# Fourier sums formed pair by pair at the end of the recurrence, and the first pair's MLP recorded ahead of the other pairs' mixing

## The chip, the cores and the metric

The kernel runs on one core of a Trainium2 chip. The metric is the device time of one execution in microseconds (us); of several executions the median is quoted. Runs of one call share a chip and the runs of the kernel before, and the three chips on which the experiments ran gave the kernel before as 784.95, 784.61 and 789.55 us, so times are compared within a chip, as ratios.

## The reference

The reference is a DeltaNet recurrence (4 batches, 8 heads, 768 steps, head size 48), followed by an FNet block on the joined heads (rows of 384): a two-dimensional Fourier transform, its real part added to the input, a normalization and an MLP of width 1536. All data are fp32.

```python
def _attn_ref(q, k, v, beta):
    k_n = k / (np.linalg.norm(k, axis=-1, keepdims=True) + 1e-06)
    state = np.zeros((B, H, D, D))
    for t in range(S):
        y[:, :, t] = einsum(q_t, state)
        v_old = einsum(state, k_t)
        state = state + b_t * outer(k_t, v_t - v_old)
# ... rows of the heads side by side: x is (4, 768, 384)
def _moe_ref(x, w_ch1, w_ch2):
    X = np.fft.fft(np.fft.fft(x, axis=1), axis=2)
    u = x + np.real(X)
    un = (u - mean(u)) / sqrt(var(u) + 1e-06)
    return u + np.maximum(un @ w_ch1, 0.0) @ w_ch2
```

## The kernel before

The sequence is cut into chunks of 64 steps, 12 chunks for each batch. Step `m` of the program does one chunk of the recurrence (`chain(m)`). Beside the recurrence run two generators: `pre` prepares the next group of chunks (transposes `pt`, products `pg`, then the triangular inversion on VectorE, which starts with a 1024-column transpose `X<-A`), and `side` does the Fourier mixing and the MLP of the batch before. Every fourth chunk begins a "quad"; a group is two quads.

Batch 0's rows lie in three tile pairs `x[T]`, each with two tiles of 128 rows. `fourier(b)` folds the pairs to sums and differences, transforms along the sequence (`pf`), along the features (`pb`), adds the result to the rows, and takes the statistics. `mlp(b)` normalizes a pair (`un`), transposes it (`ptr`, then `unT`), and multiplies by the first weight (`ph`) and the second (`po`).

Matmul results of all these stages, `pf`, `pb`, `pd`, `pt`, `ptr`, `ph` and `po`, lie in PSUM tiles of one tag, which has two buffers:

```python
def ps_one(shape, name):
    return ps.tile(shape, F32, tag="one", bufs=2, name=name)

def fourier(b):
    x = xs[b]
    F = wk.tile([128, 2, 2, S // 2], F32, tag="F", name="F")
    scr = wk.tile([128, 6 * (HD + 1)], F32, tag="scr", name="scr")
    for a in range(2):                     # part 0: sums, part 1: differences
        eo = scr[...]
        for T in range(TH):
            dve.tensor_tensor(eo[:, T], x[T][:, 0], x[T][:, 1], op=op)
        # ... fold along the features into ed (GpSimd for part 0), then six short sums z in scr
        yield
        for i in range(2):
            pf = ps_one([128, 512], "pf")
            # ... 24 matmul records for a part, z by stab
            act.activation(F[0:rows, a, i]..., pr, ACT.Copy)
    for T in range(TH):
        pb = ps_one([128, DM], "pb")
        # ... 4 matmuls, F by dtab
        for t, op in enumerate((ALU.subtract, ALU.add)):
            # ... four additions of pb to x[T][:, t]
        yield
        # ... (last pair: pd), bn_stats, bn_aggr, rstd
        norms[b, T] = mv, rstd
        yield

def mlp(b, groups):
    def transposed(g):
        # ...
        for tt in range(GT):
            dve.tensor_scalar(un, x[g][:, tt, :], mv[...], rstd[...], op0=ALU.subtract, op1=ALU.mult)
            pt = ps_one([128, KD, 128], "ptr")
            for dt in range(KD):
                tr(pt[:, dt, :], un[:, 128 * dt:128 * dt + 128], dt == 0)
            act.activation(unT[:, :, 128 * tt:128 * tt + 128], pt, ACT.Copy)
        return unT
    unT = transposed(groups[0])
    yield
    # ... ph, hT, po

def second(b):
    # ... batch 0:
        w = second_weight()     # fetches, converts and joins w2, slice by slice
        advance(w)
        run(fourier(b))         # the whole mixing of batch 0 is recorded at once
        mixed.add(b)
        yield
    channels = mlp(b, ...)
    if b == 0:
        for _ in range(KF + 1):
            advance(channels)
            advance(w, 2)
            yield
        run(w)
    yield from channels
```

The loop over the steps, where `side` is turned before `pre` and so the mixing is recorded before the first transposes of the preparation:

```python
    for m in range(NCH, STEPS):
        # ...
        for i, _ in enumerate(chain(m)):
            # ...
            if n == 0 and i == 1:
                run(side, *later)
                later.clear()
                side = second(b - 1)
            if m > NCH or i > 0:
                due[0] += 4.6 if g == 1 else PRE
                due[1] += SIDE[b]
            while max(due) >= 1.0:
                for i, gen in ((1, side), (0, pre)):
                    if due[i] >= 1.0:
                        due[i] -= 1.0
                        advance(gen)
```

## Time and profile before

| | kernel before |
|---|---|
| time | 788.09 us median of 3 runs (787.66 to 789.56) |
| span in the profile | 784.7 us |
| TensorE (PE) | 89% of the span |
| VectorE (DVE) | 48% |
| ScalarE (ACT) | 33% |
| rows of batch 0 complete | 147.2 us |
| products of the mixing (`pb`) | from 161.79 us |
| first transposes of the preparation (`pt`) | 172.17 us |
| first product with the first weight (`ph`) | 180.31 us |
| inversion starts (`X<-A`, 1024 columns) | 193.11 us |

The prediction below shows the main lines of this profile. It does not show the granted clock of TensorE in the 40 slices, which matters later; in this row a 9 is full speed or nearly so, and a slice is 19.6 us:

```profile
PEclk9999999989998999699999999899999999999999
```

The windows of the same kernel around the mixing (stretch, length, then busy us and count of PE, PE's weight loads, DVE, ACT and POOL; then granted clock, DMA share, GB/s):

```profile
158.00:165.00 7.00, 6.98 (x56) 5.62 (x56) 3.18 (x12) 2.05 (x3) 0.00 (x0) 1.00 0.28 73
165.00:174.00 9.00, 5.46 (x71) 3.82 (x70) 8.94 (x34) 2.48 (x5) 1.88 (x4) 0.82 0.28 89
174.00:182.00 8.00, 7.24 (x79) 5.51 (x81) 7.17 (x18) 6.06 (x17) 1.53 (x2) 0.78 0.37 67
```

While DVE adds (8.94 of 9 us), PE waits, and its clock falls to 0.82. And in the timeline (start, length, engine, operation, count) the products of the three pairs lie close together, with a wait of the preparation behind them:

```profile
161.79 3.46 PE L131 MATMUL pb<-dtab,F 128*128 128x193 f32 x16
166.12 1.76 PE L131 MATMUL pb<-dtab,F 128*128 128x193 f32 x8
```

A pair has 8 records of `pb`, so the first line is pairs 1 and 2 back to back and the second line is pair 3.

### The profile page before, as it was taken

How to read it: one execution, taken by the hardware profiler on the slowest of the kernel's cores; microseconds unless marked ns; L12 is line 12 of the kernel's file. 1: busy time of each engine (PE TensorE's matmuls, PEld its weight loads, DVE VectorE, ACT ScalarE, POOL GpSimd, SP SyncE). 2: the span in 40 equal slices, each digit the busy share in tenths (PEclk: the TensorE clock that was granted, in tenths of full speed). 3: DMA queues.
4: the chain of work that ended last, by engine and by line, in shares of the span. 5: the costliest groups of instructions: out<-in, count | busy, mean ns of one | idle time of the engine just before them, and what ended most of it. 6: DMA issues, size and time to landing. Idle time of an engine off the chain costs nothing.

```text
span 784.7 us, 17842 instructions
## 1 busy us (share of the span) xinstructions
PE 699.9 (89%) x7640; PEld 513.0 (65%) x7640; DVE 379.4 (48%) x952; ACT 260.0 (33%) x634; POOL 58.7 (7%) x83
## 2 busy tenths in 40 slices
PE   5852799989988997999989998999999989999997
PEld 4531687867656765786666775776767666677684
DVE  2699766575992598245961119783111146100000
ACT  3741354227436404532152540315312121021120
POOL 8020000010000001010100001010000010100000
PEclk9999999989998999699999999899999999999999
DMA  8651033225320212001202101001000000000000
GB/s 189 163 113 31 7 85 57 46 74 123 87 69 9 38 32 43 16 10 25 50 6 42 32 2 42 1 1 32 12 12 11 12 11 1 20 1 20 11 11 20
DMA packets 82447, 30.75 MB, mean 39 GB/s; under 512 B 77392, under 2 KB 78928, under 8 KB 82368
## 3 DMA queue, kind: packets, MB, share of 16 engines
q1 hardware_dynamic: 78224, 22.31, 13.8%
q0 software_dynamic: 1968, 6.91, 2.7%
q8 instruction: 60, 0.98, 0.5%
q10 hardware_dynamic: 2176, 0.39, 0.3%
q14 instruction: 19, 0.16, 0.1%
HBM read 24.87 MB, written 4.72 MB: 38 GB/s over the span
## 4 chain that ended last, share of the span: by engine, by line
PE 48%; DVE 10%; ACT 5%; issue 3%; DMA 0%; SPq 0%; POOL 0%; POOLq 0%; DVEq 0%; ACTq 0%
PE ph L131 20%; PE po L131 15%; DVE X L131 3%; PE pc L131 3%; DVE A L131 2%; PE pf L131 2%; PE pj L131 2%; ACT A L131 2%; PE pb L131 2%; ACT wt L131 1%; PE pg L131 1%; PE py L131 1%; DVE sm L131 1%; DVE x L131 1%; PE pt L131 1%
## 5 line engine op out<-in xcount | busy, mean ns | idle before, releaser
L131 PE MATMUL ph<-unT,w 128*128 128x256 f32 x864 | 213.8, 395 | 4.5 <-ACT unT L131 2.0
L131 PE MATMUL po<-w,hT 128*128 128x384 f32 x576 | 202.2, 498 | 1.7 <-ACT KQT L131 0.7
L131 PEld LDWEIGHTS ph<-unT,w 128*128 128x128 f32 x864 | 160.3, 193 | 33.7 <-ACT hT L131 3.7
L131 PEld LDWEIGHTS po<-w,hT 128*128 128x128 f32 x576 | 105.7, 191 | 68.2 <-issue 1.5
L131 ACT ACTIVATE hT<-ph 128x256 f32<-128x256 f32 x144 | 54.9, 383 | 179.6 <-PE ph L131 179.3
L131 DVE TENSOR_TENSOR x<-x,po 128x384 f32<-128x384 f32 x24 | 13.2, 552 | 112.5 <-PE po L131 112.4
L131 ACT ACTIVATE U<-pc 128x192 f32<-128x192 f32 x48 | 15.9, 331 | 110.0 <-PE pc L131 98.4
L131 ACT ACTIVATE KQT<-pt 128x256 f32<-128x256 f32 (+1 forms) x82 | 32.0, 419 | 44.9 <-PE pt L131 44.3
L131 PEld LDWEIGHTS pc<-U,wt 64*64 64x64 f32 x768 | 34.0, 163 | 19.7 <-issue 10.3
L131 PE MATMUL pg<-KQT 48*64 48x64 f32 (+1 forms) x1024 | 41.7, 309 | 5.5 <-ACT KQT L131 4.4
L131 PEld LDWEIGHTS pg<-KQT 48*64 48x64 f32 x1024 | 32.1, 178 | 20.4 <-ACT KQT L131 11.2
L131 PE MATMUL pc<-U,wt 64*64 64x48 f32 x768 | 41.2, 253 | 4.7 <-DVE U L131 2.1
L131 DVE TENSOR_TENSOR st<-st,pc 128x192 f32<-128x192 f32 x44 | 15.3, 347 | 61.0 <-PE pc L131 56.8
L131 DVE TENSOR_TENSOR U<-V,pc 128x192 f32<-128x192 f32 x48 | 16.8, 350 | 53.1 <-PE pc L131 52.9
L131 DVE TENSOR_TENSOR A<-X 128x30 f32<-128x30 f32 (+14 forms) x120 | 41.0, 342 | 2.9
L131 DVE TENSOR_TENSOR X<-X,A 128x30 f32<-128x30 f32 (+14 forms) x120 | 39.5, 329 | 2.9
L131 DVE TENSOR_TENSOR x<-x,pb 128x193 f32<-128x193 f32 (+1 forms) x96 | 26.4, 346 | 23.1 <-PE pb L131 23.1
L716 POOL DMA_INDIRECT out_dram<-x,rows_hi x12 | 12.3, 1024 | 335.9 <-DVE x L131 179.9
L131 PE MATMUL pt<-pack,kp 128*128 128x128 f32 x96 | 24.4, 349 | 10.3 <-DMA pack<-k_pack 4.8
L131 PE MATMUL pt<-pack,qp 128*128 128x128 f32 x96 | 23.4, 341 | 11.0 <-DMA qp<-in_q_dram 11.0
L131 PE MATMUL pj<-Z,A 32*64 32x64 f32 x320 | 15.0, 257 | 19.9 <-DVE Z L131 19.6
L131 ACT ACTIVATE A<-pg 128x256 f32<-128x256 f32 (+1 forms) x72 | 25.4, 378 | 21.7 <-PE pg L131 16.6
(125 smaller groups left out, 840.2 us busy)
## 6 DMA issues: line engine op xcount, KB each, us to landing
qp<-in_q_dram SPq DMA_DIRECT2D x96, 48.0 KB, 2.4
V<-in_v_dram SPq DMA_DIRECT2D x96, 48.0 KB, 2.4
kp<-in_k_dram SPq DMA_DIRECT2D x80, 48.0 KB, 2.5
w<-in_moe_w_ch_dram SPq DMA_DIRECT2D x8, 384.0 KB, 3.2
w<-in_moe_w_ch_dram POOLq DMA_DIRECT2D x6, 384.0 KB, 6.4
x<-in_moe_w_ch_dram SPq DMA_DIRECT2D x6, 384.0 KB, 3.7
x<-in_moe_w_ch_dram POOLq DMA_DIRECT2D x4, 384.0 KB, 9.2
out_dram<-x SPq DMA_DIRECT2D x8, 192.0 KB, 2.0
```

The source lines that it names most:

```text
L131: ins = getattr(self.engine, name)(*args, **kwargs)
L716: nc.gpsimd.indirect_dma_start(out=out.rearrange("b s m -> (b s) m"), out_offset=bass.IndirectOffsetOnAxis(ap=rows_hi[:, i:i + 1], axis=0) ...
```

## The change

The intent has three parts. The folds of each pair are formed as soon as the pair's rows are there, in the last steps of the recurrence (which are held in program order), all of them on VectorE, where GpSimd did a part of them before; and both parts (sums and differences) get tiles of their own, so that the second need not wait for the first. The additions after the products are six per pair, not eight. And the MLP of the first pair, its normalization and transposes, is recorded as soon as that pair's statistics are, ahead of the mixing of the other two, so that it can start early.

```diff
+        eds = [F[:, 1 - a].rearrange("p i k -> p (i k)") for a in range(2)]
+        if b == 0:
+            hT = wk.tile([128, KF, GT * 128], F32, tag="hT", name="hT").rearrange("p f t -> p (f t)")
+            zs = hT[:, 0:1158], hT[:, 1158:2316]
+        else:
+            scr = wk.tile([128, 6 * (HD + 1)], F32, tag="scr", name="scr")
+            zs = scr, scr
 ...
+        def folded(a, Ts, helped):       # the folds of the pairs Ts
+        def shifted(a):                  # the six short sums of a part
 ...
+        if b == 0:
+            for T in range(TH - 1, -1, -1):
+                folded(0, [T], False)
+                folded(1, [T], False)
+                if T > 0:
+                    yield
+            mixed_sums = [shifted(a) for a in range(2)]
 ...
+            add(x[T][:, :, 0:HD + 1], pb[:, None, 0:HD + 1].broadcast_to([128, 2, HD + 1]), ALU.add)
+            add(x[T][:, :, HD + 1:DM], pb[:, None, HD - 1:0:-1].broadcast_to([128, 2, HD - 1]), ALU.add)
             for t, op in enumerate((ALU.subtract, ALU.add)):
                 rop = ALU.add if op == ALU.subtract else ALU.subtract
-                add(x[T][:, t, 0:HD + 1], pb[:, 0:HD + 1], ALU.add)
-                add(x[T][:, t, HD + 1:DM], pb[:, HD - 1:0:-1], ALU.add)
 ...
             w = second_weight()
             advance(w)
-            run(fourier(b))
-            mixed.add(b)
-            yield
+            while (b, 0) not in norms:
+                advance(first_mixing)
         channels = mlp(b, list(range(TH if b == B - 1 else TH - 1)))
         if b == 0:
-            for _ in range(KF + 1):
+            advance(channels)            # un, ptr, unT of the first pair
+            run(first_mixing)            # then pairs 2 and 3
+            mixed.add(b)
+            yield
+            for _ in range(KF):
                 advance(channels)
                 advance(w, 2)
                 yield
 ...
+                if m in (10, 11):
+                    advance(first_mixing)
```

The order of the first weight's staging buffers is changed as well, so that the tile which now holds the sums is free in time.

More of the change, by code (lines that the diff above doesn't have):

```diff
@@ L315, in __init__ @@
             un = [wk.tile([128, PW, 2], I32, tag="unT", bufs=2, name="w64") for _ in range(2)]
-            self.stages = [hT[:, i] for i in range(4)] + un + [
-                xpairs[i].rearrange("p t (f two) -> p (t f) two", two=2).bitcast(I32) for i in range(3, 7)]
+            xp = [xpairs[i].rearrange("p t (f two) -> p (t f) two", two=2).bitcast(I32) for i in range(3, 7)]
+            self.stages = xp[0:2] + [hT[:, i] for i in range(4)] + un + xp[2:4]
             self.ops = []
@@ L728, in fourier, with widths @@
         F = wk.tile([128, 2, 2, S // 2], F32, tag="F", name="F")
-        scr = wk.tile([128, 6 * (HD + 1)], F32, tag="scr", name="scr")
-        for a in range(2):
-            op, op2 = (ALU.add, ALU.subtract) if a == 0 else (ALU.subtract, ALU.add)
-            w = HD + 1 if a == 0 else HD - 1
-            o = 1 if a == 0 else 0
-            eo = scr[:, 0:TH * DM].rearrange("p (t d) -> p t d", t=TH)
-            for T in range(TH):
+        eds = [F[:, 1 - a].rearrange("p i k -> p (i k)") for a in range(2)]
[5 more added lines that the diff above has]
+            zs = scr, scr
+            eds = eds[0], eds[0]
+        def widths(a):
+            return (HD + 1, 1) if a == 0 else (HD - 1, 0)
+        def folded(a, Ts, helped):
+            op = ALU.add if a == 0 else ALU.subtract
+            w, o = widths(a)
+            eo = zs[a][:, 0:TH * DM].rearrange("p (t d) -> p t d", t=TH)
+            ed = eds[a][:, 0:TH * w].rearrange("p (t d) -> p t d", t=TH)
+            for T in Ts:
                 dve.tensor_tensor(eo[:, T], x[T][:, 0], x[T][:, 1], op=op)
-            ed = F[:, 1].rearrange("p i k -> p (i k)")[:, 0:TH * w].rearrange("p (t d) -> p t d", t=TH)
-            eng = nc.gpsimd if a == 0 else nc.vector
-            eng.tensor_tensor(ed[:, :, o:o + HD - 1], eo[:, :, 1:HD], eo[:, :, DM - 1:HD:-1], op=op)
+            ts = slice(min(Ts), max(Ts) + 1)
+            eng = nc.gpsimd if helped else nc.vector
+            eng.tensor_tensor(ed[:, ts, o:o + HD - 1], eo[:, ts, 1:HD], eo[:, ts, DM - 1:HD:-1], op=op)
             if a == 0:
-                nc.gpsimd.tensor_copy(ed[:, :, 0:HD + 1:HD], eo[:, :, 0:HD + 1:HD])
-            z = scr[:, 0:6 * w].rearrange("p (i d) -> p i d", i=6)
+                nc.gpsimd.tensor_copy(ed[:, ts, 0:HD + 1:HD], eo[:, ts, 0:HD + 1:HD])
+        def shifted(a):
+            w = widths(a)[0]
+            ed = eds[a][:, 0:TH * w].rearrange("p (t d) -> p t d", t=TH)
+            z = zs[a][:, 0:6 * w].rearrange("p (i d) -> p i d", i=6)
             dve.tensor_tensor(z[:, 3], ed[:, 1], ed[:, 2], op=ALU.add)
@@ L749, in fourier @@
             dve.scalar_tensor_tensor(z[:, 2], z[:, 5], 0.5, ed[:, 0], op0=ALU.mult, op1=ALU.add)
-            dve.scalar_tensor_tensor(z[:, 4], z[:, 3], -0.5, ed[:, 0], op0=ALU.mult,
-                                           op1=ALU.add)
+            dve.scalar_tensor_tensor(z[:, 4], z[:, 3], -0.5, ed[:, 0], op0=ALU.mult, op1=ALU.add)
+            return z
+        if b == 0:
[5 more added lines that the diff above has]
+            mixed_sums = [shifted(a) for a in range(2)]
+        for a in range(2):
+            w = widths(a)[0]
+            if b > 0:
+                folded(a, range(TH), a == 0)
+            z = shifted(a) if b > 0 else mixed_sums[a]
             yield
@@ L908, in second @@
             advance(w)
-            run(fourier(b))
+            while (b, 0) not in norms:
+                advance(first_mixing)
+        channels = mlp(b, list(range(TH if b == B - 1 else TH - 1)))
+        if b == 0:
+            advance(channels)
+            run(first_mixing)
             mixed.add(b)
             yield
-        channels = mlp(b, list(range(TH if b == B - 1 else TH - 1)))
-        if b == 0:
-            for _ in range(KF + 1):
+            for _ in range(KF):
                 advance(channels)
@@ L979 @@
     act_work = {0: [T(1, 0)], 1: [T(1, 1)], 2: [Dg(1)], 4: [T(2, 0), Dg(2)], 6: [T(2, 1)], 8: [T(3, 0), Dg(3)], 10: [T(3, 1)]}
+    first_mixing = fourier(0)
     rest = seq(w.join(), masks(3))
```

## The prediction

> **What bounds the kernel now.** I read the page's slices first, then the windows by stage, then the timeline of the stage that the change touches, then the waits there. The page's slices of the kernel before say that TensorE (PE) is the engine to look at over most of the run, but not everywhere:
>
> ```profile
> span 784.7 us, 17842 instructions
> PE 699.9 (89%) x7640; PEld 513.0 (65%) x7640; DVE 379.4 (48%) x952; ACT 260.0 (33%) x634; POOL 58.7 (7%) x83
> PE   5852799989988997999989998999999989999997
> DVE  2699766575992598245961119783111146100000
> ```
>
> One slice is 19.6 us. The change touches slices 7 to 9 (about 135 to 185 us: end of batch 0's recurrence and batch 0's Fourier mixing). There PE shows 9, 8, 8 and VectorE (DVE) 5, 7, 5, and the slices after it (10 to 12) show DVE at 9, 9, 2. So a share of busy time over the whole run says nothing here; the stages have different limits. The view of windows gives those limits (columns: stretch, its length, then busy us and count of each engine):
>
> ```profile
> 140.00:165.00 25.00, 23.16 (x380) 20.38 (x372) 13.42 (x38) 6.11 (x13) 1.59 (x2) 1.00 0.25 50
> 165.00:180.00 15.00, 10.85 (x134) 8.08 (x132) 14.55 (x48) 6.54 (x16) 3.41 (x6) 0.77 0.32 80
> 180.00:194.00 14.00, 13.15 (x188) 10.22 (x187) 4.71 (x9) 10.95 (x32) 0.00 (x0) 1.00 0.60 143
> 194.00:240.00 46.00, 41.06 (x203) 28.04 (x201) 43.02 (x115) 17.94 (x42) 2.65 (x2) 0.96 0.30 73
> 488.00:632.00 144.00, 143.06 (x1481) 102.21 (x1476) 53.50 (x145) 37.59 (x90) 7.15 (x11) 0.98 0.05 12
> ```
>
> Read as: from 165 to 180 us DVE is full (14.55 of 15) and PE lacks 4.15 us; from 194 to 240 DVE is full again (43.0 of 46, the triangular inversion of the next group and the joining of the second weight's words) and PE lacks 4.9; from 488 on PE is full (143 of 144). Whatever is saved before 240 moves the rest forward, as far as it is on DVE's or PE's path there.
>
> The timeline of the mixing itself:
>
> ```profile
> 147.91 1.40 POOL L740 TENSOR_TENSOR F<-scr 128x573 f32<-128x573 f32 x1 [102.84 <-DVE scr L131]
> 150.55 5.07 PE L131 MATMUL pf<-stab,scr 128*128 128x65 f32 x24 [0.16 <-DVE scr L131]
> 152.14 0.56 DVE L131 TENSOR_TENSOR scr<-x 128x384 f32<-128x384 f32 x1 [0.84 <-PE pf L131]
> ...
> 158.40 3.42 PE L131 MATMUL pf<-stab,scr 128*128 128x64 f32 x24
> ...
> 163.59 2.20 DVE L131 TENSOR_TENSOR x<-x,pb 128x193 f32<-128x193 f32 x8 [3.82 <-PE pb L131]
> ...
> 172.17 0.69 PE L131 MATMUL pt<-pack,kp 128*128 128x128 f32 x2 [2.32 <-DVE x L131]
> ...
> 174.39 0.45 DVE L131 TENSOR_SCALAR un<-x,mv,rstd 128x384 f32<-128x384 f32 x1
> ...
> 180.31 1.56 PE L131 MATMUL ph<-unT,w 128*128 128x256 f32 x6 [0.16 <-ACT unT L131]
> ```
>
> The columns are start, length, engine, operation, count and the idle time before it. The last of batch 0's rows is in place at 147.2 us. Part 0's sums are folded by GpSimd (1.40), then six short sums, then its 24 matmuls; part 1's sums cannot be written into the one scratch tile before part 0's matmuls have read it (the 0.84 wait), so part 1's matmuls start at 158.40. Each pair of row tiles then costs eight additions (2.20) and statistics (1.3) on DVE, and the next group's transposes (pt) wait until 172.17 because the PSUM buffer they need is freed by the last of these additions. The MLP (ph) starts at 180.31, 33.1 us after the rows were complete.
>
> **What the Trainium skill says.** "VectorE: DVE Perf Modes", section "The TRN2 errata", gives an fp32 two-tensor addition as (N+151)/0.96 ns. For N=384 that is 557 ns, the trace has 555 (scr<-x); for 191 it is 356, the trace has 345 to 352: it agrees. "GPSIMD Engine Reference", section 3.1, gives GpSimd's addition as 1.96 times DVE's; the trace has 1.394 against 0.754 us for the same 573 columns, 1.85 times. "TensorE: Matmul & The Clock Gate", part 1, says the array runs at half clock until about 3.4 us of sustained work. The trace agrees: 24 pf matmuls took 5.07 us at 150.55 and 3.42 at 158.40, and sixteen pc matmuls 0.68 before and 0.45 after; after the thin stretch from 165 on a pair of pt took 0.69 again against 0.44 at 179.5. The page's granted-clock row reads 1.00 at 150 though the matmuls are slow, so I go by durations. "Perfetto Trace Analysis", section "Optimization Strategy", says that repeated gaps can mean that no SBUF or PSUM buffer is left; the pt wait of 2.32 on "DVE x" is such a gap.
>
> **The change, part by part.**
>
> 1. *Folding moved into steps 10 and 11.* Per pair four DVE operations: two of 384 columns and two of 191. Successive starts in the trace are 0.48 apart for the former (141.27 to 141.75) and 0.275 for the latter (2.20/8), so 2 x 0.48 + 2 x 0.275 = 1.5 us. Two pairs are folded in a stretch that is held in program order; the gap of DVE between a step's state addition (139.15) and the next step's U (140.31) has 0.9 us free, of which a mask already takes most. I charge 1.5 us to the last rows (they come at about 148.7 instead of 147.2), not 3.0, because the first-weight joining is over by 138 and DVE has 2.98 us of idle at 143.4.
>
> 2. *Last pair and the sums.* After the rows only the third pair is left: 1.5 us on DVE. It replaces the 0.6 of the last fold, GpSimd's 1.40 + 0.19 and hand-overs (147.26 to 149.59 = 2.3): saves 0.8. Then the same six sums, 1.7 us, the first usable after three (0.96).
>
> 3. *No wait between parts.* Part 1's sums lie in a tile of their own. The gap between 155.62 and 158.40 is 2.8 us, but about 2 us of it hold recurrence matmuls that must still run somewhere; I count 1.0 to 1.5 us. Only in batch 0; the other batches keep the shared scratch.
>
> 4. *Six additions for eight.* Two of about 384 columns (0.48) and four of 191 (0.275): 2.06 against 2.20, so 0.14 for each pair, 0.4 for batch 0 on DVE's full stretch. In batches 1 to 3 it lies beside PE work: nothing.
>
> 5. *First pair's MLP ahead.* Normalization, transposes and copy of pair 0 are recorded before the mixing of pairs 1 and 2. Pair 0's statistics stood at 168.3; before, `un` ran only at 174.39. With points 1 to 4 the first pair's additions end near 164, statistics at 165.2, `rstd` at 166.4, and 3.5 us of un, transposes and copies give ph near 170 instead of 180. PE's missing 4.15 us between 165 and 180 can be filled, and PE stays warm: pt and pg matmuls between 172 and 179 took 0.69 for 0.44 and 1.99 for 1.10, about 2 us in sum. Against this: DVE pays two `un` (0.9) earlier on its full stretch, so pairs 1 and 2 and the freeing of PSUM come 0.9 later relative to their start.
>
> Sum on the path to the next group's preparation: +1.5 - 0.8 - 1.2 - 0.4 + 0.9 = 0.0, then about -2 for the clock, so the inversion starts some 2 us earlier than 193.1. PE work moved into idle time gives up to 4 us more, but it can pay only where PE is later the bound (after 255 us): I count 1.6. In all -3.6: 788.1 - 3.6 = 784.5.
>
> **The rivals.**
>
> *The second weight takes the place of the wait.* The pair's second matmul (po) needs all twelve slices of the second weight, and they are joined on DVE (about 1.3 us each) until 227; a wait of po for that stands in the trace at 227.35 (0.95 us). The hidden tile has one buffer, so pair 1 cannot run ahead of po. If so, an earlier ph only makes PE wait longer between 195 and 230, and the gain is 0 to 2 us: 786 to 788. The full DVE of 194 to 240 speaks for it; that DVE is 9.3 us idle from 180 to 194, where joins could go, speaks against.
>
> *The recurrence pays.* If the folds in the ordered stretch delay steps 11 and 12 by their full 1.5 us each, and MLP evictions get in the way of the preparation on ScalarE (10.95 of 14 busy at 180 to 194), the time is 788 to 790.
>
> *The inversion starts much earlier.* If warm PE and earlier buffers bring the preparation forward by 6 us or more, all later stages move with it: 778 to 781. The 15 us of full DVE before it speaks against more.
>
> **Range and chances.** The scheduler that orders the instructions reacts to all moved work, so I widen by about 3 us on each side. Predicted 784.5 us, with 778 to 790 to hold it 8 times in 10. Over 2% faster would be under 772.3, more than all of PE's idle time in the touched stage: 0.04. Over 2% slower (above 803.9) needs a new stall of 16 us: 0.01. Within 2%: 0.95.
>
> **What would show it.** Right: folds of 384 and 191 columns between 135 and 146 us; two blocks of pf matmuls nearly back to back; the first ph before 173 us; PE above 12 of 15 us in the stretch that follows the mixing; the group's inversion (the 1024-column transpose that stands at 193.11) 1 to 4 us earlier. Wrong: that transpose unmoved or later, po waiting for the weight for several us, or a first ph still near 180.

## More of the kernel before

The preparation of the group that stands beside batch 1's first steps is *kept in program order* with respect to what was recorded before it.

## The result

The changed kernel is correct and takes **796.81 us** (795.92 to 798.33, 4 runs), against 788.83 us (787.66 to 789.62) for the kernel before on the same chip. The ratio is 1.0104, 95% interval 1.0082 to 1.0127. A ratio here is the mean time of one kernel's fast runs over that of the other's fast runs of the same rounds, so it is not quite the ratio of the medians. The time rose by some 8 us; it was predicted to fall by 3.6, and it lies outside the range of 778 to 790. The class of within 2% was right.

The head of the page of the changed kernel (span; busy time and share; the PE and clock rows of its 40 slices):

```profile
span 794.2 us, 17838 instructions
PE 704.4 (89%) x7640; PEld 514.9 (65%) x7640; DVE 378.1 (48%) x933; ACT 260.1 (33%) x634; POOL 58.7 (7%) x84
PE   5851799778998997999989998999999989999997
PEclk9999999968998999599999999899999999999999
```

The work is the same, with the same 7640 matmul records, but PE is busy 4.5 us longer. Slices 7 and 8 show PE at 7 and the clock in slice 8 at 6. The windows of the changed kernel, same stretches as before:

```profile
158.00:165.00 7.00, 3.26 (x72) 2.60 (x71) 4.28 (x13) 0.98 (x2) 0.95 (x2) 0.97 0.01 2
165.00:174.00 9.00, 9.00 (x54) 6.42 (x54) 3.57 (x11) 1.43 (x3) 0.00 (x0) 0.50 0.00 0
174.00:182.00 8.00, 7.31 (x76) 5.21 (x73) 6.89 (x22) 4.01 (x10) 1.98 (x4) 0.52 0.50 136
```

Where PE was full before (6.98 of 7) it now stands for more than half of the time, and in the 17 us after that it runs at half clock. The timeline of PE says what stood where; brackets give an idle time and what ended it:

```profile
157.69 1.76 PE L131 MATMUL pb<-dtab,F 128*128 128x193 f32 x8
...
162.86 0.67 PE L131 MATMUL pc<-U,wt 64*64 64x48 f32 x16 [2.57 <-DVE U L131]
164.69 0.87 PE L131 MATMUL ptr<-pack,un 128*128 128x128 f32 x3 [1.17 <-DVE un L131]
...
165.88 0.90 PE L131 MATMUL ptr<-pack,un 128*128 128x128 f32 x3
...
167.09 6.38 PE L131 MATMUL pb<-dtab,F 128*128 128x193 f32 x16
...
174.65 1.49 PE L131 MATMUL pd<-dtab,gz 128*32 128x193 f32 x4
176.07 0.69 PE L131 MATMUL pt<-pack,kp 128*128 128x128 f32 x2
```

The first pair's products start 4.1 us earlier than before (157.69 for 161.79): the new sums work. But the products of pairs 2 and 3, whose operand has been ready since before 159, come only after both `ptr` transposes, at 167.09, and these 16 records take 6.38 us where 16 took 3.46 before. So the preparation's first `pt` comes at 176.07, 3.9 us later than before, in spite of the earlier start. From there to the inversion it takes 24.5 us, where it took 20.9. Part of that is seen on ScalarE and PE of the changed kernel:

```profile
173.56 1.01 ACT L131 ACTIVATE wtmp<-x 128x384 int32<-128x384 uint32 x2 [6.25 <-PE pb L131]
...
189.10 0.54 ACT L131 ACTIVATE wtmp<-x 128x384 int32<-128x384 uint32 x1 [1.60 <-DMA x<-in_moe_w_ch_dram]
```

The conversion of the second weight writes into the buffer of `F`, so it waits for the last `pb` (173.56; it came at 167.98 before). Its third slice then waits for a transfer, and the evictions of the preparation queue behind it on ScalarE. The inversion starts at 200.54 instead of 193.11:

```profile
200.54 1.97 DVE L131 STREAM_TRANSPOSE X<-A 128x1024 f32<-128x1024 f32 x1
```

The shift stays to the end: the next group's inversion is also 7.4 us later (276.08 for 268.66), and the span 9.5 us longer.

### The profile page after: what moved, and what is told of

Same layout as the page of the kernel before. It is cut to its first block, busy times and chain, and to the rows that moved or that the text cites. A ratio compares the mean times of both kernels' runs of the same rounds, so it can differ in the third digit from the quotient of the medians.

```text
span 794.2 us, 17838 instructions
## 1 busy us (share of the span) xinstructions
PE 704.4 (89%) x7640; PEld 514.9 (65%) x7640; DVE 378.1 (48%) x933; ACT 260.1 (33%) x634; POOL 58.7 (7%) x84
## 4 chain that ended last, share of the span: by engine, by line
PE 47%; DVE 10%; ACT 5%; issue 3%; DMA 1%; SPq 1%; POOL 0%; POOLq 0%; DVEq 0%; ACTq 0%
PE ph L131 18%; PE po L131 15%; PE pc L131 3%; DVE X L131 3%; DVE A L131 2%; PE pf L131 2%; PE pj L131 2%; ACT A L131 2%; PE pb L131 2%; ACT wt L131 1%; PE pg L131 1%; PE py L131 1%; DVE sm L131 1%; PE ptr L131 1%; PE pt L131 1%
## 5 line engine op out<-in xcount | busy, mean ns | idle before, releaser
L131 PEld LDWEIGHTS pc<-U,wt 64*64 64x64 f32 x768 | 33.5, 161 | 24.5 <-DVE U L131 10.3
L131 DVE TENSOR_TENSOR x<-x,pb 128x191 f32<-128x191 f32 (+1 forms) x72 | 24.9, 414 | 32.4 <-PE pb L131 32.2
L131 PEld LDWEIGHTS pc<-st,KQT 48*64 48x64 f32 x768 | 19.1, 155 | 21.1 <-DVE st L131 10.6
```

The costliest lines, as they stand in the source:

```text
L131: ins = getattr(self.engine, name)(*args, **kwargs)
```

## The experiments

The theory after the result: recording the first pair's MLP ahead takes the place of the products of pairs 2 and 3; PE stands idle, its clock halves, and the preparation comes late. The rivals: the folds in the last steps delay the recurrence; or VectorE's early normalization delays the other pairs; or the second weight's transfers are to blame. First the parts were run apart, on one chip (before: 784.95 us).

### The changed kernel once more

No edit. It is the control for the chip.

> The changed kernel again, as a control on the same chip as the runs sent with it: 1.009 to 1.013 times the kernel before, as in the first measurement (1.0104).

Measured: 795.35 us, ratio 1.0123 (1.0076 to 1.0170). The loss is there again, the inversion starts at 201.41, and the clock from 165 to 174 us is 0.50 again.

### All but the MLP ahead

```diff
-            while (b, 0) not in norms:
-                advance(first_mixing)
-        channels = mlp(b, ...)
-        if b == 0:
-            advance(channels)
             run(first_mixing)
             mixed.add(b)
             yield
-            for _ in range(KF):
+        channels = mlp(b, ...)
+        if b == 0:
+            for _ in range(KF + 1):
                 advance(channels)
```

> The change without its last part: the folding by pairs, both parts' sums at once and the six additions stay, but the first pair's transposes are recorded after all mixing, as before. Theory A (TensorE is held: the transposes stand in its order ahead of the second and third pair's products, wait for the first pair's statistics, and the array then runs at half clock): 783 to 786 us, since the products of the first pair already came 4 us earlier in the changed kernel (157.7 against 161.8). Rival B (the folds in the ordered steps or the moved first-weight stages cost the time): stays at 795 to 798.

Measured: 785.28 us, ratio 1.0007 (0.9966 to 1.0048): the loss is gone. The timeline of PE and the inversion in it:

```profile
158.19 3.46 PE L131 MATMUL pb<-dtab,F 128*128 128x193 f32 x16
...
168.22 0.41 PE L131 MATMUL pt<-pack,kp 128*128 128x128 f32 x2 [2.17 <-issue]
...
190.98 1.96 DVE L131 STREAM_TRANSPOSE X<-A 128x1024 f32<-128x1024 f32 x1
```

The products come 3.6 us earlier than in the kernel before, the first `pt` 3.9, but the inversion only 2.1. An effect of about 2 us on the time lies inside the interval of 0.4% either way, so it is neither shown nor excluded.

### The MLP ahead alone

The kernel before with this part only:

```diff
-            run(fourier(b))
-            mixed.add(b)
-            yield
+            first_mixing = fourier(b)
+            while (b, 0) not in norms:
+                advance(first_mixing)
 ...
+            advance(channels)
+            run(first_mixing)
+            mixed.add(b)
+            yield
 ...
```

> The kernel before with only the last part of the change: the first pair's MLP start recorded ahead of the other pairs' mixing. Theory A: 797 to 801 us, as it has the loss of about 12 us without the 4 us won by the sums. Rival B: 788 to 790, as before.

Measured: 794.56 us, ratio 1.0126 (1.0084 to 1.0167): the whole loss, from this part by itself. (The time is below the expected 797 to 801, on a chip where the kernel before is some 4 us faster.) The same picture as in the changed kernel, 4 us later:

```profile
161.58 1.77 PE L131 MATMUL pb<-dtab,F 128*128 128x193 f32 x8
...
168.72 0.87 PE L131 MATMUL ptr<-pack,un 128*128 128x128 f32 x3 [0.89 <-DVE un L131]
...
171.12 6.38 PE L131 MATMUL pb<-dtab,F 128*128 128x193 f32 x16
```

With this pair of runs the rival of the folds in the recurrence is out: 0 and +9.6 us add up to the changed kernel's loss.

### Normalization ahead, transposes after

The changed kernel, with the two `un` of the first pair still ahead on DVE, and its six transposes on PE recorded after all mixing:

```diff
 ... (normed() and turned() are the two halves of transposed())
-        unT = transposed(groups[0])
+        if b == 0:
+            uns = normed(groups[0])      # the two un
+            yield
+            unT = turned(uns)            # ptr and unT
+        else:
+            unT = transposed(groups[0])
 ...
             advance(channels)
             run(first_mixing)
+            advance(channels)
             mixed.add(b)
```

> The changed kernel, with the first pair's normalization on VectorE still recorded ahead of the other pairs' mixing, but its transposes on TensorE after it. Theory A: the products of pairs two and three no longer stand behind the transposes, 783 to 787 us. Rival C (the harm is the MLP's early start itself, its evictions on ScalarE and weight fetches getting between the next group's preparation): 790 us or more, since the hidden layer starts as early or earlier.

Measured: 787.08 us, ratio 1.0016 (0.9976 to 1.0056). The loss is gone again, though the two `un` stand ahead on VectorE in the trace (164.73, before pair 2's last additions), so VectorE's early work is not it; the place of the transposes is. (The profiled run was the slowest of this kernel, 792.03, so its times are not used for fine differences.) Pairs 1 and 2 go back to back at 158.15, and the inversion starts at 192.03.

### Useless products in the wait

The changed kernel with eight products of 384 columns, whose results nobody reads, written into the `ptr` tiles before the transposes overwrite them:

```diff
                 pt = ps_one([128, KD, 128], "ptr")
+                if b == 0 and g == 0:
+                    for _ in range((6, 2)[tt]):
+                        mm(pt.rearrange("p c d -> p (c d)"), w1[:, 0, 0:128], w1[:, 1, 0:DM], True)
```

> The changed kernel with eight useless products of 384 columns written into the two transposes' PSUM tiles before the transposes overwrite them (about 5 us of TensorE at full clock, in the time in which it waits). Theory A with the clock as half of the loss: the second and third pair's sixteen product instructions take about 3.5 us instead of 6.4, the following transposes 0.44 instead of 0.69, and the time falls to 789 to 793. If the clock counts for nothing and only the wait does: 796 to 799.

Measured: 786.43 us, ratio 1.0022 (0.9981 to 1.0063), where the control on the same chip took 795.35. The lines that tell it:

```profile
159.97 4.78 PE L131 MATMUL ptr<-w 128*128 128x384 f32 x14
...
166.36 3.36 PE L131 MATMUL pb<-dtab,F 128*128 128x193 f32 x16
...
173.27 0.66 PE L131 MATMUL pt<-pack,kp 128*128 128x128 f32 x2 [1.94 <-issue]
```

The products of pairs 2 and 3 start nearly as late as in the changed kernel (166.36 for 167.09). Yet now they take 3.36 us, and the inversion starts at 194.59. So the wait by itself costs little; what it does to the clock costs the larger part, about 9 of the 10 us between the control and before. The order of the recurrence's matmuls moved a little too, so this share is not pure. And the profiled run was the slowest of its kernel (794.91 us; its next inversion, at 278.35, is no earlier than the control's 278.45): its lines show what became of the clock, while the gain itself is shown only by the times of the other four runs (786.2 to 788.88). The expectation was 789 to 793.

### The transposes in a PSUM tile of their own

So far the order of the instructions and the PSUM buffers moved together. The second pair's `pb` takes the buffer that the first `ptr` has held, because the tag has two buffers and the tiles take turns as recorded: pair 1's products, first `ptr`, second `ptr`, pair 2. Two later runs separate the two causes. This one is the changed kernel, recorded in the same order, with only the place of the first pair's `ptr` changed; the tag `pair` lies unused at that time:

```diff
-                pt = ps_one([128, KD, 128], "ptr")
+                if b == 0 and g == 0:
+                    if tt == 0:
+                        own = ps_pair("own", "pair")
+                    pt = own[:, tt, 0:DM].rearrange("p (c d) -> p c d", c=KD)
+                else:
+                    pt = ps_one([128, KD, 128], "ptr")
```

> The changed kernel, with one edit: the first pair's two transposed tiles lie in a PSUM tile that is otherwise unused at that time, not in the two buffers that the mixing's products take in turn. If the harm of recording the MLP ahead comes from the buffers (the second pair's products need the buffer that the first transposed tile holds), the products of pairs 2 and 3 start before 164 us instead of 167.1, run at full clock (sixteen in 3.4 to 3.6 us), the inversion starts at 190 to 194 instead of 200.5, and the time is 0.995 to 1.004 of before, like the run without the MLP ahead. If it comes from the mere order, or from the two normalizations and transposes ahead, the products stay behind the transposes and the time stays near 1.011 of before.

Measured, on a chip where the kernel before takes 789.55 us: 786.06 us (783.91 to 787.12, 6 runs), ratio 0.9954, 95% interval 0.9927 to 0.9981. The loss has become a small gain. The timeline of PE and the inversion:

```profile
157.68 3.46 PE L131 MATMUL pb<-dtab,F 128*128 128x193 f32 x16
...
161.91 1.76 PE L131 MATMUL pb<-dtab,F 128*128 128x193 f32 x8
164.80 0.55 PE L131 MATMUL own<-pack,un 128*128 128x128 f32 x3 [1.13 <-DVE un L131]
...
169.32 0.66 PE L131 MATMUL pt<-pack,kp 128*128 128x128 f32 x2 [1.94 <-issue]
...
174.83 1.46 PE L131 MATMUL ph<-unT,w 128*128 128x256 f32 x6
...
190.01 1.96 DVE L131 STREAM_TRANSPOSE X<-A 128x1024 f32<-128x1024 f32 x1
```

With the buffers apart, the scheduler puts the products of pairs 2 and 3 ahead of the transposes, though they are recorded behind them. The inversion starts 10.5 us earlier than in the changed kernel and 3.1 earlier than before. Here recording ahead was harmless in itself; the shared buffers made it harmful. (With the preparation ahead as well it is not harmless, as the last run below shows.) This agrees with the Trainium skill, "Perfetto Trace Analysis", section "Matmuls", which wants independent groups of matmuls to rotate through different PSUM banks so that the emptying of one overlaps the next group. Here the two groups did rotate, but the one in front had to wait for VectorE's `un`, and the ready one stood behind it for a buffer.

### Why the earlier sums alone gained nothing: three runs

The run without the MLP ahead had its products 3.6 us early and no shorter time. Three edits of that kernel ask why.

The first no longer records the folds in steps 10 and 11, which are held in program order, but all of them after the last rows, still in tiles of their own:

```diff
-                if m in (10, 11):
-                    advance(first_mixing)
```

> The variant without the MLP ahead, and with no folding in steps 10 and 11: all three pairs are folded at once when the last rows are there, still with both parts' sums in tiles of their own. My prediction's step 1 charged 1.5 us to the last rows for folding early and step 2 took 3 us of folding out of their way: so this should be slower than that variant by 0 to 2 us, its first sums' products starting at 150 to 152. If the early folds cost what the rival says, it is faster by 2 us or more.

Measured: 784.59 us (784.04 to 792.29), the kernel before on this chip taking 784.61; ratio 1.0022 (0.9957 to 1.0087). The products start at 157.39, which is 0.8 us *earlier* than with the folds recorded in the steps (158.19), since the rows are complete at 147.15 instead of 148.08. But this is no run without early folding. The scheduler moved the folds of two pairs forward by itself, into gaps of VectorE before the last rows; the first stands at 133.65, where the changed kernel has it at 139.87:

```profile
133.65 0.55 DVE L131 TENSOR_TENSOR hT<-x 128x384 f32<-128x384 f32 x1
```

So what costs the recurrence 0.9 us is to pin the folds to steps 10 and 11. What folding early is worth was not tested. Two things bring the products forward: the first block of `pf` starts at 149.22 for 150.55 in the kernel before, with no fold of GpSimd after the rows, and the second at 154.60 for 158.40, with a tile for each part.

The second keeps PE busy through the preparation, with six useless products pinned behind the third pair's:

```diff
             if T == TH - 1:
+                if b == 0:
+                    idle = ps_pair("idle", "pair")
+                    strict[0] = True
+                    for _ in range(6):
+                        mm(idle[:, 0, 0:DM], w1[:, 0, 0:128], w1[:, 1, 0:DM], True)
+                    strict[0] = False
```

> The variant without the MLP ahead, with six useless products of 384 columns (about 3.9 us at full clock) pinned behind the third pair's products, where TensorE waits for the additions. If the half clock between 164 and 176 is what keeps this variant from gaining: the preparation's transposes take 0.41 instead of 0.69 each, its products 1.1 instead of 1.99, the inversion starts 1 to 2 us earlier and the time falls to 0.995 to 0.999 of before. If VectorE and ScalarE set the preparation's length: no change from that variant, 1.000 to 1.003.

Measured: 787.99 us, ratio 1.0043 (1.0004 to 1.0083), not better. The clock stays at 1.00 from 165 to 182, but the inversion starts at 193.47:

```profile
182.90 1.22 PE L131 MATMUL ph<-unT,w 128*128 128x256 f32 x2 [2.31 <-ACT KQT L131]
184.05 1.99 PE L131 MATMUL pg<-KQT 48*64 48x128 f32 x32
```

PE waits 2.31 us for ScalarE, which stands behind a slice of the second weight, and comes out of it at half clock (32 `pg` take 1.99; at full clock they take 1.10). With the MLP not ahead, the clock of the first transposes does not set the preparation's length; this trace points to ScalarE and these transfers, which the next run moves.

The third moves the second weight's conversions three turns later:

```diff
-            for _ in range(KF + 1):
+            for k in range(KF + 1):
                 advance(channels)
-                advance(w, 2)
+                if k >= 3:
+                    advance(w, 2 if k > 3 else 8)
```

> The variant without the MLP ahead, with the second weight's slices after the first two converted on ScalarE only after the next group's preparation (same work, three steps later). Theory: in that variant ScalarE waits 1.15 us for a slice's transfer in front of the preparation's evictions, and with the conversions (about 3 us) out of the way the inversion starts 2 to 3 us earlier, at about 188; the time then is 0.994 to 0.998 of before. Rival: the hidden layer's second product then waits for the weight and the gain is given back, 0.999 to 1.004.

Measured: 787.12 us (one of four runs, 796.37, slow), ratio 1.0018 (0.9952 to 1.0083). The inversion starts 1.7 us earlier than without this edit (189.30 for 190.98), but the transpose `Z` that closes it starts 1.3 us later (236.54 for 235.21; 236.92 in the kernel before). From 189 to 237 us VectorE now spends 17.06 us on the weight's words instead of 13.03, and is busy for 46.05 of 48 us. What was won at the start of the inversion was given back in it.

### The preparation recorded before the mixing

These runs pointed at the place of the preparation. It stands behind the whole mixing, while ScalarE is busy for 6.1 of 25 us from 140 to 165. So the kernel without the MLP ahead was given one more edit, which records the preparation's 6 stages of one quad, or all 12, before the mixing:

```diff
                 due[1] += SIDE[b]
+            if m == NCH and i == 1:
+                advance(pre, 12)
             while max(due) >= 1.0:
```

Half of it:

> The variant without the MLP ahead, with the first quarter of the next group's preparation (six steps, one of its two quads) recorded before the mixing instead of after it. Theory: the next group's inversion is what all later stages wait for, and ScalarE is idle during the mixing (6 of 25 us busy), so the inversion starts 4 to 8 us earlier and the time falls to 0.990 to 0.996. Rival: the mixing is delayed by as much as the preparation is brought forward, 0.998 to 1.003.

Measured: 781.91 us, ratio 0.9950 (0.9909 to 0.9991); inversion at 183.49.

All of it:

> The same with both quads prepared (twelve steps) before the mixing. Theory: the inversion follows the mixing directly, 8 to 14 us earlier; 0.984 to 0.993. Rival: mixing, hidden layer and second weight are all delayed by about 10 us and TensorE lacks work later, 0.998 to 1.006.

Measured: **774.23 us** (771.78 to 774.35), ratio **0.9851** (0.9812 to 0.9891), the best version: 1.5% faster than before. A window and two lines of its timeline:

```profile
140.00:165.00 25.00, 20.76 (x412) 18.08 (x408) 15.62 (x38) 13.95 (x40) 0.82 (x3) 1.00 0.38 67
```

```profile
162.82 1.95 DVE L131 STREAM_TRANSPOSE X<-A 128x1024 f32<-128x1024 f32 x1
...
165.94 3.46 PE L131 MATMUL pb<-dtab,F 128*128 128x193 f32 x16
```

ScalarE is busy for 13.95 of the 25 us, and the inversion starts 30 us earlier, before the mixing's products. Its end, `Z`, comes 15 us earlier (222.03): the mixing's additions and the inversion now share VectorE (28.6 of 30 us busy from 165 to 195).

Is the rest of the change needed for that? The same edit on the kernel before, and on the changed kernel:

> The kernel before, with nothing but both quads of the next group's preparation recorded ahead of the mixing. If the gain of 1.5 per cent of the combined variant is the preparation's alone: 0.985 to 0.989. If the early sums contribute once the preparation is out of the way: 0.990 to 0.994, as the first products come about 3 us later.

Measured: 784.56 us, ratio 0.9984 (0.9941 to 1.0027). Neither expected range was met. The inversion starts early (163.78), but the products come at 173.54: part 1's sums wait 2.80 us for part 0's `pf` in the one scratch tile, and then share VectorE with the inversion. `Z` starts at 230.11.

> The changed kernel as it is, with the MLP ahead, and both quads of the preparation recorded ahead of the mixing. Theory: the transposes hold TensorE's queue, and that hurt because the preparation stood behind them; with the preparation in front, the early MLP costs little or nothing: 0.982 to 0.989. If the MLP ahead does harm in itself (half clock for the pairs' products, VectorE's order): 0.992 to 1.000.

Measured: 783.29 us, ratio 0.9970 (0.9930 to 1.0010). The products of pairs 2 and 3 are again held and at half clock:

```profile
167.23 1.77 PE L131 MATMUL pb<-dtab,F 128*128 128x193 f32 x8
...
176.41 6.38 PE L131 MATMUL pb<-dtab,F 128*128 128x193 f32 x16
```

So the gain needs products that are not held, and it needs the rest of the change; which of its parts (tiles of their own, folds on VectorE, fewer additions) was not tested one by one.

The last run is the changed kernel with both edits, the preparation ahead and the transposes in a tile of their own:

> The same edit together with the next group's two preparations recorded ahead of the mixing. That pair of edits without the PSUM edit gave 0.997 of before, and without the MLP ahead 0.985. If the buffers are the harm, this run comes to 0.983 to 0.990, products of pairs 2 and 3 are no longer at half clock behind transposes; if not, it stays at 0.995 to 1.0.

Measured: 786.53 us where before takes 789.55, ratio 0.9952 (0.9907 to 0.9996). The expectation of 0.983 to 0.990 was missed. The products do go well (pairs 1 and 2 from 166.21 in 3.46 us), and the inversion is as early (163.10, `Z` at 223.63), but the next group's inversion starts at 263.44, where the best version has 252.80. PE's granted clock from 195 to 300 us is 0.85 here, 0.97 there. The trace shows where the two part: PE waits 4.49 us for `Z` here, while the best version still has `po` to do until 225.29; and from 225 to 255 us, with PE busy for 29.25 of 30 us here and 29.24 there, the clock is 0.52 here and 1.00 there, and 361 matmul records get done instead of 539.

```profile
225.70 1.74 PE L131 MATMUL pj<-Z,A 32*64 32x64 f32 x32 [4.49 <-DVE Z L131]
```

So the idle time and the half clock come back at another place. That the early MLP causes this, having taken away the work that filled the wait, is likely but not tested. With the preparation ahead, recording the MLP ahead does not help: 0.9952 against 0.9851, on different chips, but with intervals that do not meet.

## Why the prediction was wrong

Right were the following steps.

- *Part 3, no wait between the parts.* The second block of `pf` starts 4.99 us after the first in the changed kernel (149.91, 154.90) and 7.85 us after it before (150.55, 158.40): 2.9 us, where 1.0 to 1.5 were counted. The recurrence's matmuls, which were thought to need that room, went into waits of PE.
- *Part 2, the last pair.* From the last rows to the first `pf` 2.07 us against 3.32: 1.25 saved, where 0.8 were counted.
- *Part 4, six additions.* 2.07 against 2.20 us: 0.13, where 0.14 were counted. This part was not run alone.
- *Part 1, the folds' cost to the last rows* was sized too high: 0.6 us (147.84 for 147.23), not 1.5. The run with the folds recorded last shows that even this was paid for pinning them.

**The step that failed is part 5**, the first pair's MLP ahead. It charged 0.9 us, for the two `un` on VectorE, and expected the first `ph` near 170, PE filled, and 2 us gained from a warm clock. Measured: the products of pairs 2 and 3 delayed by 7.7 us (they could have followed pair 1's at 159.4 and started at 167.09), the clock at half until 182, and the first `ph` at 181.69, later than before. The prediction did name the resource, "pairs 1 and 2 and the freeing of PSUM come 0.9 later" (it counts the pairs from 0), and quoted the page on buffers for the `pt` wait, but it did not write down the order in which the tiles take the two buffers. Had it done so, it would have seen that pair 2's products need the buffer of a transpose, and that this transpose has to wait for the first pair's products, additions, statistics, `rstd` and `un`: from 157.69 to 164.69 in the trace.

The sign of the clock term was wrong by consequence: the idle time cooled PE, and the run with useless products shows that most of the loss passes through the clock. None of the three rivals named this. The second-weight rival is seen in part in the longer preparation, but not as a wait of `po` (for the weight PE waits 0.27 us there in the changed kernel, 0.34 before); "the recurrence pays" had the right direction and the wrong cause.

That the buffers are the failed term is shown by the run with the tile of its own. It gives 0.9954 of before; the prediction, 784.5 for 788.1, was 0.9954. The inversion starts 3.1 us earlier, where "some 2" was predicted and 1 to 4 given as the sign. The agreement should not be read too finely, since its terms are not right one by one: the first `ph` is at 174.83, not 170, and the `pt` and `pg` that were to be warm still run at half clock (0.66 and 1.98 us). Three readings of the prediction need correction, though its sum does not rest on them. It gave PE's slices 7 to 9 as 9, 8, 8 and VectorE's slices 10 to 12 as 9, 9, 2; the rows that it shows read 9, 8, 9 and 5, 9, 2. The 0.95 us at 227.35 is the wait of PE's weight load; the products themselves waited 0.34. And it says that the trace agrees with some 3.4 us of work lifting the clock: but sixteen `pc` take 0.68 us from 128 us on until 155.5, with PE busy for 9.47 of the 10 us from 120 on, so this thin work did not lift it, and the granted clock reads 1.00 all that time. What made the same matmuls faster at 158 us (0.45) the trace does not show.

## What to carry to other kernels

When work is recorded earlier, write out which tiles share its buffers and in which order they take them: a tile whose input comes late, put ahead of one that is ready, holds the ready one although no data connect them. A stretch in which TensorE half idled was charged twice here, once as the wait and again as half clock in the work behind it (3.46 and 6.38 us for the same 16 records), so look for the same instruction's duration before and after. And before work is moved within a stage, ask which stage's end moves everything after it: here that was the next group's preparation, and putting it first gave, on top of the change without its early MLP, the 1.5% that the change itself did not.

## What the Trainium skill lacked or had wrong

- "TensorE: Matmul & The Clock Gate", part 1, gives the array half clock after an idle window of about 3.4 us, and full clock after a busy one. Here no idle time of that length came before: the two waits were 2.57 and 1.17 us, with thin matmuls between, 3.26 of 7 us busy. And after it PE was busy for 9.00 of 9.00 us, 6.38 of them with ordinary products, yet the clock read 0.50 there and 0.52 in the 8 us that followed, in the changed kernel (0.50 in both in its repetition); in the run with both edits it read 0.52 over 30 us with PE busy for 29.25. How busy TensorE must be to be counted as such is not on the page.
- "Perfetto Trace Analysis", section "Matmuls", advises rotation through different PSUM banks. It lacks the case where two stages rotate through the same two banks and the stage in front is late: 7.7 us of delay for products that were ready, gone when the late tiles got a place of their own.
- The skill advises to keep TensorE busy, by the order of loops or by padding a thin operand, but no page of it that was read fills a wait with useless products: some 5.6 us of them brought the time from 795.35 to 786.43 us on one chip.
- "GPSIMD Engine Reference", section 3.1, has 1.96 times VectorE's time for an addition of 2048 columns; the trace of the kernel before has 1.85 for 573 columns (1.394 against 0.754 us).
